# Attention with a mixture of experts on one core: an opening with earlier loads, moved constants, shift rows on another queue and cleared products on TensorE

## The chip, the core and the metric

One core of a Trainium2 chip runs the whole program. The metric is the device time of one execution in microseconds (us), lower is better. The engines are TensorE (PE; its weight loads are listed apart as PEld), VectorE (DVE), ScalarE (ACT), GpSimd (POOL) and SyncE (SP, which here only issues DMAs). ACT also issues DMAs, on a queue of its own.

## The reference

```python
scores = scale * np.matmul(q, k.transpose(0, 1, 3, 2))        # 8 x 8 heads, 576 positions, 64 channels
cum = np.cumsum(np.maximum(s, 0.0), axis=-1)
bias = -(cum[:, :, :, None] - cum[:, :, None, :])
scores = np.where(causal, -1000000000.0, scores + np.minimum(bias, 0.0))
scores = scores - np.max(scores, axis=-1, keepdims=True)
attn = np.exp(scores); attn = attn / (np.sum(attn, axis=-1, keepdims=True) + 1e-09)
x = (attn @ v) with heads side by side, 4608 x 512
# each of the 4608 rows goes to the best of 4 groups and in it to the best of 4 experts
out[rows] = g_w * e_w * (np.maximum(x[rows] @ w1[g, e], 0.0) @ w2[g, e])
```

## The kernel before, in words

The 64 heads are taken in 32 pairs, p = 0 to 31 in the code (so the "fourth pair" is p = 3), and head n belongs to pair n // 2. A step of the main loop of `attention` handles three heads at once: the row maxima of head step + 4 (`rowmax`, `LEAD = 4`), the scores of head step (`scores`) and the product with V of head step - 1 (`av`). Steps -4 to -1 hold only row maxima, step 0 row maxima and scores. The attention is followed by the experts (`moe`), in which TensorE multiplies with weights that are streamed in.

For each pair the raw q and k are loaded (`load_raw`, L159, tile `r`, three buffers). ACT rounds them to fp32r (`split`, L166, tile `hl`), POOL (DVE for p = 0) takes the rests (L170). For the first pairs ACT also writes a part straight into place (`place`, L182). SP then copies the pieces into two operand tiles: `WA` (`load_a`, L191, L193; four buffers) holds rounded q and k and, in rows 64 to 67, sums of s and the shift by the row maximum; `WB` (`load_b`, L203, L204; five buffers) holds the rests. `load_v` (L207) brings V into `VT`, two buffers.

`rowmax` multiplies 66 rows of `WA` on PE (L228) into PSUM tiles `pm`; DVE masks and reduces each (L236) into `mc`. After both heads of a pair, PE transposes `mc` (L250), DVE makes the two shift rows `th` and `tl` (L256, L257) and two DMAs write them to rows 66 and 67 of `WA` (`send`, L262, issued by ACT). Only then can `scores` run for the pair: it multiplies 68 rows of `WA` (L284) and 128 rows of `WB` (L286) into tiles `ps`, ACT takes the exponential (L294), POOL clears the upper triangle (L303), and `av` multiplies with V (L326), whose results ACT copies out (L331, L334).

Each engine executes its own list in order. The lists of PE, DVE, ACT and POOL are written out by hand in strings such as `FIRST` and `ORDERS` (a letter pops one piece of pending work from a queue of that name, B2 is the third piece of the scores); the table `pre` adds loads of the first pairs behind steps -2 to 1. Up to step 0 SP's list is by hand too, later a scheduler places SP's DMAs. A DMA that is issued from SP or ACT takes the next of eight semaphores (DMAHW0 to DMAHW7), and its issuing engine first waits until the earlier DMA on that semaphore has landed:

```python
for r, t in ((66, th), (67, tl)):
    nc.scalar.dma_start(WA[i][r:r + 1, QA]...., t.bitcast(F32))
```

At the start DVE makes the running sums of s (L530 to L534, tiles `cl`, `ch`), and SP copies two rows of them per head into `WA` (L193). Constants of the routing are made by `Router.__init__` on POOL and by `Router.operands` on DVE (L745 to L757), one piece at a time between the row maxima of steps 1 to 3. `hold` adds a wait on another instruction's end, `behind` only an order on the same queue.

Of the kernel before, what the change touches and what calls it, by code (L numbers as in the profile page):

```python
# [121 lines left out]
def attention(tc, qk, v, s, wr, xs, st):  # L122
# [3 lines left out]
    with ExitStack() as ctx:  # L126
# [82 lines left out]
        def rowmax(n):  # L209
# [11 lines left out]
            def item(j, q0, rows, w, c0, cw):  # L221
# [3 lines left out]
                else:  # L225
# [292 lines left out]
        cumd = dr.tile([BH, 2, S], F32, name="cumd")  # L518
        nc.sync.dma_start(s0, s.rearrange("b h s -> (b h) s"))
# [9 lines left out]

        nc.vector.tensor_scalar(out=r1, in0=s0, scalar1=0.0, scalar2=8.0, op0=ALU.max, op1=ALU.mult)  # L530
# [164 lines left out]
class Router:  # L695


    def __init__(self, tc, ac, sm, end, ps_t, ps_s, wr_f, wr_sb, xs, st):
# [35 lines left out]
        n1 = iota("n1", [[S, B], [P, NB]], base=1, cm=1, dt=I32)  # L734
        self.part = ac.tile([P, 2, B, NB], F32, name="part")
        ni = ac.tile([P, B, NB], I32, name="ni")
        self.n1, self.ni, self.uf, self.onesf = n1, ni, uf, onesf
# [1060 lines left out]
```

## Time and profile before

| | |
|---|---|
| median of 3 runs (lowest, highest) | 870.36 us (866.64, 871.6) |
| the profiled execution, its time | 869.25 us |
| its span from first to last instruction | 867.4 us |
| mean granted TensorE clock in it | 0.996 |
| PE busy, PEld busy | 839.2 us (97%), 771.9 us (89%) |
| DVE, ACT, POOL busy | 718.4 us (83%), 615.0 us (71%), 602.5 us (69%) |

The profile shows one execution. Shares of busy time are means over very different stages, so the stages of the opening are read one by one below. [...] DMA share is the mean busy share of the 16 DMA engines, and it can come out slightly above 1.

### The profile page before, as it was taken

The page shows a single profiled execution, that of the slowest core. Times are in us where ns is not written, and L with a number is a line of the kernel's source. Part 1 is how long each engine was busy: PE and PEld are TensorE (multiplying, and loading weights), DVE is VectorE, ACT ScalarE, POOL GpSimd, SP SyncE. Part 2 cuts the span into 40 slices and gives each one's busy share as a digit, 9 for nine tenths or more (in the row PEclk, how much of TensorE's full clock was granted, in tenths as well). Part 3 has the DMA queues.
Part 4 walks back from the last instruction along what each step waited for, and adds up shares of the span by engine and source line. Part 5 has one row for each costly group of instructions (what it writes and reads, how often), then busy time and mean ns, then how long its engine had stood idle before and what let it go on. Part 6 is the DMA issues. An engine that isn't in the chain of part 4 may idle for free. (4 is left out here: it accounts for less than half of the span.)

```text
span 867.4 us, 17805 instructions
## 1 busy us (share of the span) xinstructions
PE 839.2 (97%) x5601; PEld 771.9 (89%) x5601; DVE 718.4 (83%) x1982; ACT 615.0 (71%) x1393; POOL 602.5 (69%) x745
## 2 busy tenths in 40 slices
PE   4989999999999999999999999999999999999997
PEld 2778888888888888887789999999999999999996
DVE  7657788797878889787859799989999999999972
ACT  5668778786878778777747666776677777778760
POOL 9767677676876769545867756776677777777760
PEclk9999999999999999999999999999999999999999
DMA  7899898897979888633646645655566565666620
GB/s 197 266 233 250 234 235 232 213 248 194 248 209 245 236 221 225 177 87 122 194 149 225 245 151 208 205 164 193 201 201 216 188 216 195 223 228 214 215 96 26
DMA packets 82405, 174.06 MB, mean 201 GB/s; under 512 B 9692, under 2 KB 45660, under 8 KB 74112
## 3 DMA queue, kind: packets, MB, share of 16 engines
q1 hardware_dynamic: 72192, 153.20, 60.2%
q0 software_dynamic: 7488, 18.89, 5.7%
q10 hardware_dynamic: 2624, 0.76, 0.4%
q8 instruction: 46, 0.75, 0.3%
q14 instruction: 55, 0.45, 0.2%
HBM read 108.97 MB, written 19.69 MB: 148 GB/s over the span
## 5 line engine op out<-in xcount | busy, mean ns | idle before, releaser
L1067 POOL TENSOR_TENSOR wl<-raw,wh 128x512 fp32r<-128x512 f32 x163 | 209.8, 1299 | 82.5 <-ACT wh L1064 54.6
L236 DVE CUSTOM_DVE_ANT_0 mx<-pm,mask 128x192 bf16<-128x192 f32 (+4 forms) x320 | 127.3, 418 | 33.1 <-PE pm L228 30.4
L1064 ACT CAST wh<-raw 128x512 fp32r<-128x512 f32 x256 | 154.3, 616 | 0.0
L1189 PE MATMUL ph<-xh,wh 128*128 128x256 f32 (+13 forms) x512 | 140.2, 300 | 0.1
L1189 PE MATMUL ph<-xl,wh 128*128 128x256 f32 (+13 forms) x512 | 137.7, 300 | 0.1
L228 PE MATMUL pm<-WA 66*128 66x288 f32 (+4 forms) x384 | 123.8, 355 | 14.0 <-DMA WA<-ch 9.7
L284 PE MATMUL ps<-WA 68*128 68x320 f32 (+4 forms) x384 | 135.4, 356 | 1.7 <-DMA WA<-tl 1.6
L326 PE MATMUL po<-pt,VT 128*128 128x256 f32 (+3 forms) x512 | 119.0, 351 | 3.6 <-POOL pt L303 1.8
L1196 ACT ACTIVATE hh<-ph 128x256 fp32r<-128x256 f32 (+13 forms) x128 | 53.5, 418 | 85.5 <-PE ph L1189 83.3
L1269 PE MATMUL py<-hh,wh 128*128 128x256 f32 (+13 forms) x448 | 113.4, 302 | 0.1
L1269 PE MATMUL py<-hl,wh 128*128 128x256 f32 (+13 forms) x448 | 112.5, 301 | 0.0
L286 PE MATMUL ps<-WB 128*128 128x320 f32 (+4 forms) x384 | 110.2, 300 | 0.0
L1322 DVE STREAM_TRANSPOSE yr<-yT 32x384 f32<-32x384 f32 (+1 forms) x208 | 104.6, 503 | 4.5 <-ACT yT L1266 0.3
L326 PE MATMUL po<-pu,VT 128*128 128x320 f32 (+1 forms) x384 | 105.2, 382 | 0.0
L1159 DVE STREAM_TRANSPOSE xt<-xg 32x256 f32<-32x256 f32 (+1 forms) x208 | 102.3, 492 | 2.7
L326 PEld LDWEIGHTS po<-pt,VT 128*128 128x128 f32 x512 | 87.8, 191 | 16.6 <-POOL pt L303 2.5
L1189 PEld LDWEIGHTS ph<-xh,wh 128*128 128x128 f32 x512 | 95.3, 189 | 0.6 <-DVE hl L1197 0.3
L1189 PEld LDWEIGHTS ph<-xl,wh 128*128 128x128 f32 x512 | 94.7, 189 | 0.5 <-DVE xl L1142 0.3
L1189 PE MATMUL ph<-xh,wl 128*128 128x256 f32 (+13 forms) x512 | 91.9, 299 | 0.0
L170 POOL TENSOR_TENSOR WB<-r,hl 64x576 fp32r<-64x576 f32 x62 | 88.0, 1420 | 5.5 <-ACT hl L166 1.7
L228 PEld LDWEIGHTS pm<-WA 66*128 66x128 f32 (+1 forms) x384 | 68.9, 192 | 24.0 <-POOL WA L528 9.6
L422 POOL TENSOR_TENSOR xTl<-xT,xTh 128x512 fp32r<-128x512 f32 x29 | 37.0, 1275 | 75.9 <-ACT xTh L417 55.7
(255 smaller groups left out, 2001.0 us busy)
## 6 DMA issues: line engine op xcount, KB each, us to landing
raw<-in_w_dram SPq DMA_DIRECT2D x64, 1024.0 KB
r<-in_qk_dram SPq DMA_DIRECT2D x32, 576.0 KB
WA<-hl SPq DMA_DIRECT2D x60, 288.0 KB
WB<-hl SPq DMA_DIRECT2D x60, 288.0 KB
VT<-in_v_dram SPq DMA_DIRECT2D x32, 384.0 KB
WB<-hl SPq DMA_DIRECT2D x64, 144.0 KB
xs<-xr SPq DMA_DIRECT2D x15, 512.0 KB
WA<-cumd SPq DMA_DIRECT2D x56, 4.5 KB
```

The costliest lines, as they stand in the source:

```text
L170: (nc.vector if p < 1 else nc.gpsimd).tensor_tensor(out=hl[:, 2] if part else WB[p % NBB][0:64, KA, h], in0=r[hr, part], in1=hl[hr, part]. ...
L228: nc.tensor.matmul(ps[:rows, :cw], WA[i][0:66, QA, h, QO + q0:QO + q0 + rows], WA[i][0:66, KA, h, QO + c0:QO + c0 + cw], start=True, stop= ...
L236: nc.vector.tensor_tensor_reduce(out=tmp[:rows, :cw], in0=ps[:rows, :cw], in1=mk[:rows], scale=1.0, scalar=-3.0e38 if c0 == 0 else mo, op0 ...
L284: nc.tensor.matmul(ps[:rows, o:o + w], WA[i][0:68, KA, h, QO + k0:QO + k0 + rows], WA[i][0:68, QA, h, QO + q0:QO + q0 + w], start=True, st ...
L286: nc.tensor.matmul(ps[:rows, o:o + w], WB[p % NBB][:, KA, h, k0:k0 + rows], WB[p % NBB][:, QA, h, q0:q0 + w], start=False, stop=True)
L326: nc.tensor.matmul(po[0][:, qa - base:qb - base], VT[p % NVT].rearrange("p t a d -> p (t a d)")[:, (3 * t + 1 + h) * 64:][:, 0:P], x[:, c: ...
L1064: self.casts.append(nc.scalar.copy(h[:, j], raw[:, j]))
L1067: self.low = lows[self.u, i, j] = nc.gpsimd.tensor_tensor(out=l[:, j], in0=raw[:, j], in1=h[:, j].bitcast(F32), op=ALU.subtract)
L1159: V.transpose(dst[:, 0:n, :, j], src[:, 0:n, :, i])
L1189: self.product = nc.tensor.matmul(pss[f][:, :cap], w[f // 4][:, c, (f % 4) * P:(f % 4 + 1) * P], x[:, c, :cap], start=(c == 0 and w is sel ...
L1269: self.product = nc.tensor.matmul(pss[c][:, :cap], w[2 + f // 4][:, f % 4, c * P:(c + 1) * P], x[:, f, :cap], start=(f == 0 and w is self. ...
L1322: V.transpose(dst[:, 0:n, :, i], src[:, 0:n, :, j])
```

## The change

It edits six things, all in the first twelve microseconds of the program or in the first few steps.

- A zero tile `still` is made by DVE, and `stir(n)` multiplies it with itself n times on PE: bf16, 128 rows, 512 columns, into a PSUM tile that nobody reads. 16 such products stand at the head of PE's list, 4 behind ACT's rounding of the sums, and one behind every product of the row maxima of heads 0 to 3.
- The raw load of p = 3 is issued before the `WB` copies of p = 0, its `place` and `split` go ahead of step 0 on ACT, and `load_a(3)` follows its rests.
- The rounding of the sums goes from DVE to ACT, ahead of ACT's other casts; `place(0, 0)` goes behind the two `split` of p = 0.
- The four small DVE operations that make `part` go from steps 2 and 3 to the head of DVE's list, with their POOL input; the casts of `ub` and `ob` go from DVE to ACT.
- The shift rows of p = 2 to 5 (and the second row of p = 0) are issued by SP instead of ACT.
- The `WB` copies of p = 5 wait for an exponential of head 4 and stand behind the `WA` row copies of that pair.

```diff
-                nc.sync.dma_start(w[64:66, KA, h, QO:].bitcast(F32), (cumh if p < 4 else cumd)[n:n + 1].bitcast(F32))
+                st.at["wa", p] = nc.sync.dma_start(w[64:66, KA, h, QO:].bitcast(F32), (cumh if p < 4 else cumd)[n:n + 1].bitcast(F32))
...
+                copies = [nc.sync.dma_start(w[0:64, QA, h], hl[hr, 1])] if h or not placed else []
+                copies.append(nc.sync.dma_start(w[64:128, b, h], hl[hr, 0::2][:, b]))
+                for i in copies if p == 5 else ():
+                    hold(tc, i, st.at["exp", 4])
+                    behind(tc, i, st.at["wa", p])
...
+                if n < LEAD:
+                    stir(1)
...
-                    nc.scalar.dma_start(WA[i][r:r + 1, QA].bitcast(F32).rearrange("o h q -> o (h q)"), t.bitcast(F32))
+                    (nc.sync if (p == 0 and r == 67) or 2 <= p <= 5 else nc.scalar).dma_start(WA[i][r:r + 1, QA].bitcast(F32).rearrange("o h q -> o (h q)"), t.bitcast(F32))
...
+        still = ac.tile([P, P], BF16, name="still")
+        nc.vector.memset(still, 0.0)
+        stirred = ps_o.tile([P, 512], F32, name="stirred", tag="po").rearrange("p (a c) -> p a c", c=P)
+
+        def stir(n):
+            for _ in range(n):
+                i = nc.tensor.matmul(stirred, still, still.unsqueeze(1).to_broadcast([P, 4, P]), start=True, stop=True)
+            return i
+
+        stir(16)
...
+        nc.gpsimd.iota(n1, pattern=[[S, B], [P, NB]], base=1, channel_multiplier=1, allow_small_or_imprecise_dtypes=True)
+        for k, x, op in ((0, 6, ALU.arith_shift_right), (1, 63, ALU.bitwise_and)):
+            nc.vector.tensor_scalar(out=ni, in0=n1, scalar1=x, scalar2=None, op0=op)
+            nc.vector.tensor_copy(part[:, k], ni)
...
-        nc.vector.tensor_copy(cumh[:, 0], c2)
+        rounded = nc.scalar.copy(cumh[:, 0], c2)
+        hold(tc, stir(1), rounded)
+        stir(3)
...
-        pre = {-2: [(load_a, 2, True)],
-               -1: [(load_b, 1, True), (load_v, 0), (load_raw, 3), (load_raw, 4)],
-               0: [(place, 3, 0), (split, 3, 0), (split, 3, 1), (load_a, 3, True), (place, 3, 1), (place, 3, 2), (load_v, 1)],
+        pre = {-2: [(load_a, 2, True), (place, 3, 0), (split, 3, 0, True), (split, 3, 1, True), (place, 3, 1), (place, 3, 2)],
+               -1: [(load_b, 1, True), (load_v, 0), (load_raw, 4)],
+               0: [(need, "G", 3), (load_a, 3, True), (load_v, 1)],
...
-        V.tensor_copy(self.ub, self.uf)
-        yield
-        V.tensor_copy(self.ob, self.onesf)
...
+        self.tc.nc.scalar.copy(self.ub, self.uf)
+        yield
+        self.tc.nc.scalar.copy(self.ob, self.onesf)
```

What stands in the lists now is shown at three places. The first is the head of PE's list, where `pm0` and `pm1` are the row-maximum products of heads 0 and 1. Before, it read:

```order
L228 MATMUL pm0_4_0_235<-WA0_107 128x288
L228 MATMUL pm0_0_0_239<-WA0_107 64x64
L228 MATMUL pm0_1_0_243<-WA0_107 128x192
L228 MATMUL pm0_2_0_247<-WA0_107 128x320
L228 MATMUL pm0_3_0_251<-WA0_107 128x448
```

In the changed kernel the twentieth zero product is followed by these rows (each zero product also loads its weights):

```order
L529 MATMUL stirred_132<-still_130 128x512
L230 MATMUL pm0_4_0_264<-WA0_107 128x288 [waits DMAHW5_49,Activation_49,Pool_49]
L529 LDWEIGHTS still_130
L529 MATMUL stirred_132<-still_130 128x512
L230 MATMUL pm0_0_0_269<-WA0_107 64x64
```

So 16 + 4 zero products stand ahead of the first useful one, and 24 more alternate with the 24 products of heads 0 to 3; behind the last of them nothing of the kind follows.

The second place is SP's list between the `WA` copies of p = 1 and those of p = 2; the digit behind a tile's name is the pair, or for `WA`, `WB` the buffer. Before:

```order
L193 DMA WA1_108<-ch_127 2x1x576 [waits DMAHW2_49]
L204 DMA WB0_111<-hl0_171 64x2x576 [waits DMAHW3_49,DVE_49]
L203 DMA WB0_111<-hl0_171 64x576 [waits DMAHW4_49]
L204 DMA WB0_111<-hl0_171 64x576 [waits DMAHW5_49]
L193 DMA WA2_109<-ch_127 2x1x576 [waits DMAHW6_49,Pool_49]
```

Now:

```order
L193 DMA WA1_108<-ch_127 2x1x576 [waits DMAHW2_49]
L159 DMA r3_223<-in_qk_dram 128x1152 [waits DMAHW3_49,DVE_49,Activation_49]
L203 DMA WB0_111<-hl0_201 64x2x576 [waits DMAHW4_49]
L202 DMA WB0_111<-hl0_201 64x576 [waits DMAHW5_49]
L203 DMA WB0_111<-hl0_201 64x576 [waits DMAHW6_49]
L202 DMA WB2_113<-hl2_252 64x576 [waits DMAHW0_49,Activation_49]
L266 DMA WA0_107<-tl0_332 1x10x128 [waits DMAHW1_49,DVE_49]
L193 DMA WA2_109<-ch_127 2x1x576 [waits DMAHW2_49,Pool_49]
```

The load of p = 3 and one `WB` copy of p = 2 have come in, and the second shift row of p = 0 stands behind them.

The third place is SP's list around the shift rows of p = 3. Before, they stood in ACT's list and SP went from V and the raw load straight on to the `WB` copies of p = 5. Now:

```order
L203 DMA WB4_115<-hl4_543 64x2x576 [waits DMAHW3_49]
L209 DMA VT0_116<-in_v_dram 128x6x128 [waits DMAHW4_49,PE_49]
L159 DMA r7_790<-in_qk_dram 128x1152 [waits DMAHW5_49]
L191 DMA WA1_108<-hl5_625 64x2x576 [waits DMAHW6_49,PE_49]
L193 DMA WA1_108<-cumd_129 2x576 [waits DMAHW7_49]
L159 DMA r8_962<-in_qk_dram 128x1152 [waits DMAHW0_49,Pool_49]
L266 DMA WA3_110<-th3_758 1x10x128 [waits DMAHW1_49,DVE_49]
L266 DMA WA3_110<-tl3_759 1x10x128 [waits DMAHW2_49,DVE_49]
L193 DMA WA2_109<-cumd_129 2x576 [waits DMAHW3_49,PE_49]
L202 DMA WB0_111<-hl5_625 64x576 [waits DMAHW4_49,Activation_49]
```

The two shift rows stand behind the raw load of p = 8 and ahead of the `WB` copies of p = 5.

## Rows read from the trace of the kernel before

**Rows 1.** The page: busy time by engine, and PE in 40 slices.
```profile
PE 839.2 (97%) x5601; PEld 771.9 (89%) x5601; DVE 718.4 (83%) x1982; ACT 615.0 (71%) x1393; POOL 602.5 (69%) x745
...
PE   4989999999999999999999999999999999999997
```

**Rows 2.** Busy time by stretch: stretch, length, PE, PEld, DVE, ACT, POOL, PEclk, DMA share, GB/s.
```profile
9.65:22.20 12.55, 9.35 (x25) 5.87 (x26) 10.63 (x51) 6.64 (x10) 12.07 (x22) 1.00 0.82 200
...
22.20:27.90 5.70, 5.52 (x22) 4.80 (x23) 2.81 (x13) 3.04 (x7) 4.06 (x8) 1.00 1.04 352
27.90:34.40 6.50, 6.50 (x29) 5.76 (x30) 2.55 (x13) 5.03 (x12) 5.50 (x9) 1.00 0.80 234
34.40:41.40 7.00, 6.34 (x36) 4.71 (x34) 6.33 (x18) 4.79 (x12) 5.11 (x8) 1.00 0.90 249
41.40:47.90 6.50, 5.62 (x33) 4.56 (x33) 5.99 (x21) 5.17 (x12) 5.91 (x9) 1.00 0.93 229
47.90:55.35 7.45, 5.65 (x36) 4.74 (x34) 4.43 (x16) 3.10 (x8) 4.24 (x5) 1.00 0.98 239
55.35:62.38 7.03, 7.03 (x37) 6.32 (x37) 3.52 (x14) 6.26 (x16) 3.51 (x6) 0.76 0.90 223
62.38:67.90 5.52, 5.52 (x35) 4.86 (x34) 3.63 (x13) 4.03 (x11) 4.59 (x7) 1.00 0.91 219
```

**Rows 3.** Matmuls by shape, L286 with 448 columns: 22.2 to 31.3, 32 to 52.
```profile
L286 PE MATMUL ps<-WB 128*128 128x448 f32 x1 | 0.6, 575 | 0.0
...
L286 PE MATMUL ps<-WB 128*128 128x448 f32 x4 | 1.5, 369 | 0.0
```

**Rows 4.** Busy time by stretch again, for the 3.35 us behind PE's gap.
```profile
55.35:58.70 3.35, 3.35 (x12) 3.04 (x13) 1.00 (x5) 2.71 (x7) 0.23 (x1) 0.50 0.86 251
```

**Rows 5.** Instructions in order of time, the lead-in: start, us, engine, line, tiles, [idle before].
```profile
4.17 0.50 DVE L530 TENSOR_SCALAR cl<-cl 64x576 f32<-64x576 f32 x1 [4.17 <-DMA cl<-in_s_dram]
...
6.08 0.74 DVE L533 CAST ch<-cl 64x576 fp32r<-64x576 f32 x1
...
6.71 2.41 ACT L166 CAST hl<-r 128x576 fp32r<-128x576 f32 x4
...
9.65 0.95 PE L228 MATMUL pm<-WA 66*128 66x288 f32 x3 [9.65 <-DMA WA<-ch]
```

**Rows 6.** The same view: DVE's set-up operations, first and last of six, and POOL beside them.
```profile
36.58 1.43 DVE L749 CAST ub<-uf 128x128 bf16<-128x128 f32 x1
...
43.42 0.18 DVE L757 CAST part<-ni 128x40 f32<-128x40 int32 x1
...
36.52 2.89 POOL L170 TENSOR_TENSOR WB<-r,hl 64x576 fp32r<-64x576 f32 x2 [1.74 <-ACT hl L166]
```

**Rows 7.** The same view, the shift rows of p = 0 and the first scores.
```profile
18.07 0.74 ACTq L262 DMA_DIRECT2D WA<-tl  x1
...
22.21 0.55 PE L284 MATMUL ps<-WA 68*128 68x256 f32 x1 [1.57 <-DMA WA<-tl]
```

**Rows 8.** The same view, ACT from 16 to 31 us.
```profile
23.01 0.38 ACT L294 ACTIVATE pt<-ps 128x256 f32<-128x256 f32 x1 [6.65 <-PE ps L286]
```

**Rows 9.** The same view, the shift rows of p = 3 and what stands around them.
```profile
46.16 0.49 SPq L203 DMA_DIRECT2D WB<-hl  x1
...
50.44 0.75 ACTq L262 DMA_DIRECT2D WA<-th  x1
...
54.10 0.73 ACTq L262 DMA_DIRECT2D WA<-tl  x1
...
55.35 1.19 PE L326 MATMUL po<-pt,VT 128*128 128x256 f32 x2 [1.80 <-issue]
```

**Rows 10.** DMA issues by line: count in the program, size of one.
```profile
r<-in_qk_dram SPq DMA_DIRECT2D x32, 576.0 KB
WA<-hl SPq DMA_DIRECT2D x60, 288.0 KB
...
VT<-in_v_dram SPq DMA_DIRECT2D x32, 384.0 KB
```

More of the change, by code (lines that the diff above doesn't have):

```diff
@@ L201, in load_b @@
                 b = slice(1 if placed and h else 0, 2)
-                if h or not placed:
-                    nc.sync.dma_start(w[0:64, QA, h], hl[hr, 1])
-                nc.sync.dma_start(w[64:128, b, h], hl[hr, 0::2][:, b])
+                copies = [nc.sync.dma_start(w[0:64, QA, h], hl[hr, 1])] if h or not placed else []
[3 more added lines that the diff above has]
+                    behind(tc, i, st.at["wa", p])
         def load_v(p):
@@ L528, in ones @@
                 nc.gpsimd.memset(WA[i][64:66 if a == QA else 68, a].bitcast(F32).rearrange("p h q -> p (h q)"), 1.0)
+        n1, ni = (ac.tile([P, B, NB], I32, name=n) for n in ("n1", "ni"))
+        part = ac.tile([P, 2, B, NB], F32, name="part")
+        nc.gpsimd.iota(n1, pattern=[[S, B], [P, NB]], base=1, channel_multiplier=1, allow_small_or_imprecise_dtypes=True)
+        for k, x, op in ((0, 6, ALU.arith_shift_right), (1, 63, ALU.bitwise_and)):
+            nc.vector.tensor_scalar(out=ni, in0=n1, scalar1=x, scalar2=None, op0=op)
+            nc.vector.tensor_copy(part[:, k], ni)
         nc.vector.tensor_scalar(out=r1, in0=s0, scalar1=0.0, scalar2=8.0, op0=ALU.max, op1=ALU.mult)
         nc.vector.tensor_tensor_scan(out=c2, data0=r1, data1=r1, initial=0.0, op0=ALU.add, op1=ALU.max)
-        nc.vector.tensor_copy(cumh[:, 0], c2)
+        rounded = nc.scalar.copy(cumh[:, 0], c2)
+        hold(tc, stir(1), rounded)
+        stir(3)
         nc.vector.tensor_tensor(out=cumh[:, 1], in0=c2, in1=cumh[:, 0].bitcast(F32), op=ALU.subtract)
@@ L551, in attention @@
         ones(2)
-        place(0, 0)
         split(0, 0)
         split(0, 1)
+        place(0, 0)
         load_a(0, True)
@@ L561, in attention @@
         load_a(1, True)
+        load_raw(3)
         load_b(0, True)
-        rt = Router(tc, ac, late, end, small, ring, wr_f, wr_sb, xs, st)
+        rt = Router(tc, ac, late, end, small, ring, wr_f, wr_sb, part, xs, st)
         place(1, 1)
@@ L695, with __init__ @@
 class Router:
-    def __init__(self, tc, ac, sm, end, ps_t, ps_s, wr_f, wr_sb, xs, st):
+    def __init__(self, tc, ac, sm, end, ps_t, ps_s, wr_f, wr_sb, part, xs, st):
         self.end = end
@@ L732, in __init__ @@
         nc.gpsimd.iota(st.ie, pattern=[[1, E]], base=0, channel_multiplier=0, allow_small_or_imprecise_dtypes=True)
[L734 to L737, printed above, removed]
+        self.part, self.uf, self.onesf = part, uf, onesf
     def operands(self):
-        V, ni, n1 = self.tc.nc.vector, self.ni, self.n1
+        V = self.tc.nc.vector
         G = self.tc.nc.gpsimd
@@ L743, in operands @@
         G.memset(self.real[64:P, 20:25], 0.0)
-        yield 5
+        yield 6
+        self.tc.nc.scalar.copy(self.ub, self.uf)
+        yield
+        self.tc.nc.scalar.copy(self.ob, self.onesf)
+        yield 4
         V.tensor_copy(self.wr_sb[:, :, 0:20], self.wr_f)
@@ L747, in operands @@
                         op=ALU.subtract)
-        yield
-        V.tensor_copy(self.ub, self.uf)
-        yield
-        V.tensor_copy(self.ob, self.onesf)
-        yield
-        V.tensor_scalar(out=ni, in0=n1, scalar1=6, scalar2=None, op0=ALU.arith_shift_right)
-        V.tensor_copy(self.part[:, 0], ni)
-        yield
-        V.tensor_scalar(out=ni, in0=n1, scalar1=63, scalar2=None, op0=ALU.bitwise_and)
-        V.tensor_copy(self.part[:, 1], ni)
     def step(self, now=False):
```

## The prediction

> **What bounds the kernel now.** I read the page first: PE is busy for 97% of the span, and in 40 slices it is below nine tenths only in the first two and the last [rows 1]. From about 62 us on PE is therefore the bound, and time taken out of the opening passes to the end nearly one for one. The opening is where PE has time to lose, so I read it stage by stage, in the view of busy time by stretch [rows 2], cut at the start of each step's first score or V product.
>
> From 9.65 to 22.20 us only row maxima run: DVE is busy for 10.63 of 12.55 us and sets the pace, PE waits for it. Steps 0 to 5 then take 5.70, 6.50, 7.00, 6.50, 7.45 and 7.03 us, while step 6, the first undisturbed one, takes 5.52 with PE busy throughout. Steps 0 and 1 hold less work than step 6 and yet are longer. What is wrong there is the clock, and the clock column hides it: it says 1.00 from the start, but the same product of 448 columns takes 575 ns in 22.2 to 31.3 us and 369 ns later [rows 3]. In the one stretch where the column does show 0.50, the 3.35 us after PE stood still for 1.80 us [rows 4], the other products also have their slow durations. [...]
>
> **The lead-in, +0.2 us.** The first product waits for the sums' copy until 9.65; DVE starts on s at 4.17 when it lands [rows 5]. The change puts four small DVE operations ahead. They stand among six set-up operations, from 36.58 to 43.42, which take 1.43, 0.78, 1.11, 1.01, 0.94 and 0.18 us; the first ends when POOL's operation beside it does, and the last shows what such an operation takes undisturbed [rows 6]. The four need 0.7 us undisturbed (4 x 0.18) and 3.24 as the trace has them. With a start near 1.4 us (POOL's iota comes first) they end between 2.1 and 4.6 us, so the delay is 0 to 0.5 us; I take 0.2. The rounding costs 0.74 us on DVE and 0.60 on ACT (four casts in 2.41 us) [rows 5], for a second hand-over between engines: 0, with -0.1 to +0.3. `place(0, 0)`, now behind the rounding and two splits, ends near 9.1 us (6.1 + 3 x 0.6 + 1.2 for twice the columns), still ahead of 9.65. The 20 zero products run in PE's idle lead-in: 0.
>
> **The row maxima, +0.4 us.** 24 zero products of 512 columns stand between 24 useful ones. [...] DVE is busy for 10.63 us over four heads, 2.66 each [rows 2]. [...]
>
> **The start of step 0, -1.2 us.** PE waits 1.57 us for the second shift row of p = 0, issued by ACT at 18.07 and landed at 22.2 [rows 7]. On SP it no longer queues behind the first in ACT's list, but behind 720 KB of `WB` copies and a raw load. Those are issued at about 12 to 15 us and should land by 18 to 19 at the 200 to 350 GB/s of that time [rows 2]. 0 to -1.57.
>
> **The clock in steps 0 and 1, -4.1 us.** 9.2 us run at the low clock; at the high one PE needs half, a saving of 4.6 at most. Step 0 then meets DVE (2.81 us busy) and ACT (3.04) [rows 2], so I take 5.70 to 3.35, and 3.5 of step 1's 6.50 us halved: -2.35 - 1.75. This needs the casts of p = 3 out of the way: six times 576 columns, 3.6 us at 0.60 [rows 5]. In steps 0 and 1 ACT is busy for 3.04 + 5.03 = 8.1 us, as long as the two halved steps. They go to ACT's idle 6.65 us ahead of 23.0 [rows 8], if the load of p = 3 has landed by 17 us. If not, they delay the first exponential, and the saving shrinks to 2.
>
> **DVE in steps 2 and 3, -1.5 us.** The six set-up operations (5.45 us) leave DVE, which is busy for 6.33 of 7.00 and 5.99 of 6.50 us. Against 2 x 5.52 the two steps have 2.46 us to give; PE is idle for 1.54 of it [rows 2]. ACT takes two casts of 128 columns, well below 0.6 us each, with over a microsecond free per step. 0 to -2.4.
>
> **The gap at 53.5 us, -3.5 us.** ACT issues the first shift row of p = 3 at 50.44 and the second only at 54.10, and nothing that stands behind it in ACT's list runs before that; PE stops for 1.80 us for lack of what ACT should have cleared [rows 9]. DVE had made both rows by 50.8, so the wait is one for a DMA semaphore: the transfer on it left SP at 46.16 and had 7.9 us to land. That is a backlog on SP's queue. With the rows on SP, ACT is free: -1.85, and PE's 3.35 us at half clock [rows 4] become 1.7: -1.65. 0 (the wait returns elsewhere) to -3.5.
>
> **What is late next, +3 us.** Shift rows on SP stand behind that same backlog. Ahead of those of p = 3 stand, counting from the last `WB` copy of p = 4: 288 KB, V, two raw loads and a `WA` copy, 2112 KB or 2.16 MB [rows 10]. A full DMA moves 244 to 277 GB/s (239 at a share of 0.98, 249 at 0.90), so that is 7.8 to 8.9 us. In the trace the rows are made 2.5 us into step 4 and needed at step 6, 2 x 5.52 - 2.5 = 8.5 us later [rows 2, 9]. This is a draw, with up to 2 us of wait. For p = 4 and 5 another 3.0 to 3.3 MB each come between, 11 to 13.5 us of DMA against 11 us of PE. I take 1 us for each of the three pairs; 0 to 8 in all (2 for the first, up to 3 for each of the others).
>
> [...]
>
> The held copies of p = 5 are 864 KB that no longer stand ahead of these rows; they are needed at step 10, more than 20 us later: 0.
>
> **The sum.** 0.2 + 0.4 - 1.2 - 4.1 - 1.5 - 3.5 + 3 = -6.7 us. The profiled execution took 869.25 us, 1.1 below the median of the runs; 869.25 - 6.7 = 862.6 there, and 870.36 - 6.7 = **863.7 us** against the median.
>
> **The rivals.** A measurement of this kernel can tell about 0.5% (4.4 us) from no change, so faster means below 866.0 and slower above 874.7.
>
> *Shift rows behind the backlog* (0.22). The clock and ACT are won, but pairs 4 to 6 wait for their rows on SP, 8 us together instead of 3: 868.7. For it: the backlog in the trace [rows 9]. Against it: SP's list moves earlier with the rest, and 864 KB are held back. [...]
>
> *DMA paces the opening* (0.12). The DMA share is 0.80 to 1.04 in all stretches from 22 us on, and no byte is saved; PE runs ahead, then waits for V, `WA` or the raw loads, or ACT waits for a semaphore at p = 6, whose rows are still ACT's. All but about 1 us is given back: 869.4. Against it: the share falls to 0.80 in step 1, so there is room [rows 2].
>
> *The zero products hold PE up* (0.08). They don't raise the clock, or it falls in PE's idle 1 to 2 us ahead of the first useful product, as it did behind the gap of 1.80 us. [...]
>
> *All of it, no new wait* (0.13): -6.7 - 3 = -9.7: 860.7.
>
> **How the numbers follow.** My forecast has 0.45, the rivals 0.22, 0.12, 0.08 and 0.13. Faster: 0.45 + 0.13 + a tenth of the first rival, 0.60; slower 0.07; same 0.33. The range of 859 to 870.5 us leaves out the third rival, part of the last and the far end of the second: under 0.2.
>
> **What would show it.** Right: products of 448 columns at 369 ns in the first scores; the first score product near 21 us; no ACT pause between shift rows of p = 3; steps 0 to 5 of about 3.4, 4.8, 6, 6, 6 and 6 us. Wrong: 575 ns there; L228's products waiting behind zero products with DVE idle in the row maxima; PE waits for DMA `WA<-tl` at steps 6, 8 and 10, each of over 2 us; a PE gap that brings the 0.50 back.

## The result and the profile after

The changed kernel takes 877.94 us (median of 8 runs, 872.77 to 879.13), the kernel before 870.98 us on the same chip: a ratio of 1.0072, 95% interval 1.0047 to 1.0096, by the ratio 6.3 us slower (4.1 to 8.4), where 6.7 us faster was forecast. The profiled execution took 879.13 us and is the slowest of the eight; its span is 877.4 us against 867.4 before, so the two traces lie further apart (10.0 us) than the two kernels.

Busy time by stretch in the changed kernel, cut at the starts of the steps like [rows 2] (columns as there):

```profile
9.99:21.11 11.12, 9.83 (x50) 5.28 (x50) 10.48 (x51) 9.65 (x14) 10.70 (x20) 1.00 0.81 196
21.11:25.30 4.19, 3.45 (x21) 2.73 (x21) 2.57 (x13) 3.52 (x8) 4.07 (x6) 1.00 0.81 210
25.30:27.30 2.00, 0.86 (x5) 0.63 (x6) 0.66 (x4) 0.96 (x3) 2.00 (x5) 0.76 1.02 324
27.30:34.39 7.09, 7.09 (x25) 6.15 (x26) 2.06 (x9) 1.89 (x4) 4.91 (x9) 0.59 1.05 271
34.39:41.34 6.95, 6.05 (x36) 4.59 (x34) 3.59 (x16) 6.34 (x16) 4.71 (x6) 1.00 0.88 211
41.34:46.41 5.07, 5.07 (x33) 4.56 (x33) 3.51 (x13) 3.51 (x9) 4.92 (x7) 1.00 0.94 251
46.41:54.33 7.92, 5.81 (x36) 4.84 (x34) 6.52 (x20) 5.11 (x12) 5.22 (x9) 1.00 0.96 229
54.33:61.52 7.19, 5.86 (x36) 4.95 (x37) 3.54 (x14) 5.04 (x13) 3.70 (x6) 1.00 0.85 201
61.52:67.31 5.79, 5.53 (x34) 4.69 (x34) 4.06 (x15) 4.17 (x10) 4.44 (x6) 1.00 0.88 208
67.31:73.18 5.87, 5.87 (x36) 4.92 (x36) 3.92 (x16) 4.64 (x13) 2.94 (x4) 1.00 1.05 234
73.18:77.68 4.50, 0.00 (x1) 0.04 (x1) 0.00 (x0) 0.45 (x2) 0.76 (x3) 0.98 1.06 186
77.68:86.17 8.49, 8.49 (x33) 7.49 (x34) 3.82 (x13) 3.91 (x9) 3.95 (x6) 0.61 0.91 247
```

Step 0 starts at 21.11 us, 1.1 sooner than before, and takes 4.19 us for 5.70. Step 1 (25.30 to 34.39) takes 9.09 for 6.50 and gives all of it back: step 2 starts at 34.39, as before. Step 3 is shorter (5.07 for 6.50), step 4 longer (7.92 for 7.45). In this trace the loss is made in step 7, with 4.50 us in which PE does nothing, and in step 8 behind it, which runs at half clock (granted 0.50) up to 84.0 us and has a mean of 0.61 over its 8.49 us. Before, the same two steps read:

```profile
67.90:73.30 5.40, 5.40 (x39) 4.89 (x37) 4.35 (x18) 4.75 (x14) 2.81 (x6) 1.00 0.87 238
73.30:78.70 5.40, 5.40 (x35) 4.74 (x34) 3.52 (x13) 4.09 (x11) 5.20 (x8) 1.00 1.01 281
```

That is +4.97 and +3.09 us; step 9 starts 7.5 us later than before, and this passes unchanged to the end of the attention.

What PE waits for in 21 to 90 us of the changed kernel (engine, line, tile, what it waits for: us in total, times, longest):

```profile
PE ps L288 <- DMA WA<-tl: 5.8, 2, 4.5
...
PE po L330 <- DMA VT<-in_v_dram: 3.5, 3, 2.1
```

The longest of these waits, in order of time: PE's transpose of the maxima of p = 4, DVE's two shift rows, SP's list, and PE's next score product.

```profile
63.31 0.27 PE L254 MATMUL pmt<-ident,mc 128*10 128x128 f32 x1
...
63.94 0.28 DVE L261 SCALAR_TENSOR_TENSOR tl<-pmt,th 10x128 fp32r<-10x128 f32 x1
...
65.92 0.72 SPq L203 DMA_DIRECT2D WB<-hl  x1
66.69 1.14 SPq L159 DMA_DIRECT2D r<-in_qk_dram  x1
67.93 0.82 SPq L266 DMA_DIRECT2D WA<-th  x1
68.86 0.76 SPq L266 DMA_DIRECT2D WA<-tl  x1
...
77.68 0.55 PE L288 MATMUL ps<-WA 68*128 68x256 f32 x1 [4.50 <-DMA WA<-tl]
```

The row is made at 64.2, issued at 68.86, behind copies and a raw load in SP's list, and PE goes on some 8.8 us later: 13.5 us for 5 KB. (When it landed is taken from the end of PE's wait.)

The clock rose early, as meant, and fell again. Products of 448 columns in 20 to 27 us and in 28 to 33 us (mean ns of one last ahead of the idle time), to be read with [rows 3]:

```profile
L290 PE MATMUL ps<-WB 128*128 128x448 f32 x1 | 0.4, 367 | 0.0
...
L290 PE MATMUL ps<-WB 128*128 128x448 f32 x1 | 0.6, 575 | 0.0
```

Between them PE waits for V of p = 0, which SP issued at 22.31 us, 18.67 before; this is the product it waited with:

```profile
27.30 1.19 PE L330 MATMUL po<-pt,VT 128*128 128x256 f32 x2 [1.09 <-DMA VT<-in_v_dram]
```

### The profile page after: what moved, and what is told of

It reads as the page before. It is cut to its first block, busy times and chain, and to the rows that moved or that the text cites. A ratio compares the mean times of both kernels' runs of the same rounds, so it can differ in the third digit from the quotient of the medians.

```text
span 877.4 us, 17899 instructions
## 1 busy us (share of the span) xinstructions
PE 847.8 (97%) x5645; PEld 773.7 (88%) x5645; DVE 720.7 (82%) x1980; ACT 616.5 (70%) x1396; POOL 600.9 (68%) x745
## 5 line engine op out<-in xcount | busy, mean ns | idle before, releaser
L1081 POOL TENSOR_TENSOR wl<-raw,wh 128x512 fp32r<-128x512 f32 x163 | 209.3, 1296 | 81.8 <-ACT wh L1078 53.5
L1210 ACT ACTIVATE hh<-ph 128x256 fp32r<-128x256 f32 (+13 forms) x128 | 53.5, 418 | 85.8 <-PE ph L1203 84.5
L307 POOL TENSOR_SCALAR_AFFINE_SELECT pt<-pt 128x128 f32<-128x128 f32 (+2 forms) x192 | 65.4, 353 | 37.5 <-ACT pt L298 35.4
```

The lines of the kernel that those rows point to most:

```text
L1081: self.low = lows[self.u, i, j] = nc.gpsimd.tensor_tensor(out=l[:, j], in0=raw[:, j], in1=h[:, j].bitcast(F32), op=ALU.subtract)
```

## The experiments

The theories, as the expectations name them: A, the rows that SP issues stand behind the backlog of its queue; B, the transfers as a whole pace the opening, so that one wait only takes the place of another; C, the zero products cost time; D, the held copies of p = 5 keep SP's list standing; O, the zero products cost by what they change in the scheduler's order of SP's list.

Ratios are to runs of the kernel before on the same chip. The last four columns are from each profiled execution: how much later (+) or sooner (-) than before (36.00, 64.33, 86.17 and 379.10 us) PE transposes the maxima of p = 2, 4, 6 and 30.

| run | ratio (95% interval) | p=2 | p=4 | p=6 | p=30 |
|---|---|---|---|---|---|
| the change | 1.0072 (1.0047, 1.0096) | 0.0 | -1.0 | +7.4 | +7.4 |
| e1 change, rows on ACT | 1.0055 (1.0038, 1.0073) | -0.4 | -3.9 | +2.9 | +2.9 |
| e4 as e1, V sooner | 1.0059 (1.0032, 1.0086) | -2.2 | -1.7 | +4.3 | +4.3 |
| e5 change, no hold | 1.0092 (1.0071, 1.0114) | +0.2 | -3.2 | +4.5 | +4.4 |
| e6 change, old loads of p = 3 | 1.0080 (1.0053, 1.0107) | +1.7 | +1.4 | +4.8 | +4.6 |
| e8 change, no zero products | 1.0018 (0.9998, 1.0038) | -0.4 | -4.4 | -0.9 | -0.4 |
| e9 change, load of p = 6 sooner | 1.0082 (1.0053, 1.0111) | -2.1 | -4.4 | +1.8 | +1.8 |
| e10 change, 20 zero products | 1.0035 (1.0014, 1.0056) | -0.6 | -1.6 | +2.8 | +2.8 |
| e12 as e8, load of p = 6 late | 1.0024 (1.0000, 1.0048) | +0.1 | -3.1 | +3.7 | +3.6 |
| e13 as e8, old loads of p = 3 | 1.0038 (1.0021, 1.0055) | +2.4 | -2.6 | +2.9 | +4.2 |
| e14 as e8, no hold | 1.0015 (0.9998, 1.0032) | -0.8 | -3.7 | -1.4 | -0.2 |
| e2 before, rows of p = 2 to 5 on SP | 0.9971 (0.9953, 0.9989) | -0.2 | -3.9 | -1.6 | -1.6 |
| e18 before, rows of p = 3 on SP | 0.9988 (0.9971, 1.0004) | +0.5 | -3.2 | -2.0 | -2.1 |
| e11 as e2, constants moved | 0.9989 (0.9967, 1.0011) | +1.3 | -3.7 | -3.0 | -2.9 |
| e16 as e2, second row of p = 0 | 1.0034 (1.0016, 1.0051) | +3.2 | -1.2 | +1.4 | +1.4 |
| e3 before, zero products | 1.0028 (1.0009, 1.0047) | -0.2 | -2.2 | -2.2 | -1.6 |
| e7 as e3, one more PSUM tile | 1.0026 (1.0009, 1.0042) | +0.4 | -2.5 | -1.8 | +0.2 |
| e15 as e2, zero products | 1.0024 (1.0006, 1.0042) | +3.2 | -0.4 | +5.4 | +7.0 |
| e17 as e3, 12 more of them | 1.0032 (1.0015, 1.0050) | -0.8 | +2.1 | +2.1 | +2.0 |

Most runs are 1 to 4 us ahead at p = 4, and most of these give part or all of it back by p = 6. From there to p = 30 all but five stay within 0.5 us of where they were.

A profiled execution is one of several, and those of one kernel lie up to 10 us apart (867.06 to 877.07 us in e15). So a trace shows what can happen in a kernel, and only the ratios, which also take out the difference between chips (the kernel before has medians of 868.62 to 870.98 us on them), show what an edit is worth.

### The shift rows: e1, e2, e18

e1 undoes the rows of p = 2 to 5 in the changed kernel (e2 adds them to the kernel before, e18 those of p = 3 alone):

```diff
-(nc.sync if (p == 0 and r == 67) or 2 <= p <= 5 else nc.scalar).dma_start(WA[i][r:r + 1, QA]
+(nc.sync if p == 0 and r == 67 else nc.scalar).dma_start(WA[i][r:r + 1, QA]
```

> The changed kernel with the shift rows of pairs 2 to 5 issued by ACT again, nothing else. Theory A (rows behind the backlog of SP's queue): the wait of 4.50 us at step 8 and the half clock behind it (8.49 us instead of some 5.5) go, 7.5 us together, and ACT's stall between the rows of p = 3 comes back with up to 3.5 us: 870 to 874 us, with PE waiting for a shift row nowhere over 1 us. Theory B (the transfers as a whole pace the opening, whoever issues the rows): PE then waits for V or another copy instead, and the time stays at 876 to 880. Theory C (the zero products cost it): 876 to 880 too, with the waits for shift rows gone from steps 6 and 8 but step 10 starting no sooner than 90 us.

Measured 873.94 us. As a time that is in A's range, but by the ratios (1.0055 against 1.0072) it is 1.5 us below the change, and the intervals overlap: no gain is shown. The wait for a row is gone, but the stall of ACT is back, now at p = 4: it does nothing for 6.31 us. PE stands still behind it for 4.58 us and then runs at half clock (0.57 us for 448 columns at 70.1 us), so one stop has taken the place of the other. ACT and PE in order of time in e1:

```profile
66.65 0.72 ACTq L266 DMA_DIRECT2D WA<-th  x1
67.47 0.72 ACTq L266 DMA_DIRECT2D WA<-tl  x1
68.24 0.38 ACT L338 ACTIVATE sums<-po 64x256 f32<-64x256 f32 x1 [6.31 <-DMA WA<-th]
...
68.72 1.19 PE L330 MATMUL po<-pt,VT 128*128 128x256 f32 x2 [4.58 <-ACT sums L338]
```

> The kernel before with only the shift rows of pairs 2 to 5 moved from ACT to SP. Theory A: ACT's stall of 3.3 us at 50.4 us and the half clock behind it go (-3.5 us), and a wait for a shift row of p = 4, of 3 to 5 us, with half clock for some 8 us behind it, comes in its place (+6 to +8): 873 to 876 us, step 8 waiting for the second row. Theory B: within 1.5 us of the kernel before, 869 to 872, since the rows come as late as the other transfers do. Theory C: faster by the stall, 866 to 868.

Measured 866.88 us, 2.5 below the kernel before by the ratio, as C expected; A is wrong here. ACT's stall is gone, and the longest wait for a row, at step 8, is 1.42 us, with no half clock behind it (granted 1.00 from 71 to 80 us). SP and PE in e2, in order of time:

```profile
63.75 0.76 SPq L262 DMA_DIRECT2D WA<-tl  x1
...
71.25 0.36 PE L284 MATMUL ps<-WA 68*128 68x256 f32 x1 [1.42 <-DMA WA<-tl]
```

The rows are issued 5 us sooner than in the change and land within 7.5 us.

> The kernel before with the shift rows of p = 3 alone on SP. If ACT's stall between the two rows of p = 3, and the half clock behind it, are what the move of the rows gains (prediction's term for the gap at 53.5 us, -3.5): as with the rows of pairs 2 to 5, 866 to 867.5 us. Rival: the stall moves on to the rows of p = 4, still ACT's, as in the changed kernel with its rows back on ACT (6.3 us there): 868 to 871.

Measured 868.47 us, the rival's time, though not by its mechanism: the stall did not move to p = 4 (ACT issues those two rows at 63.32 and 64.17). In the trace it gains 2.1 us by p = 30, e2 1.6, so p = 3 alone can hold the gain, but the ratios don't settle it.

### The zero products: e8, e3, e7, e15, e10, e17

e8 takes all 44 out of the change, e3 adds them to the kernel before:

```diff
-        stir(16)
...
-        hold(tc, stir(1), rounded)
-        stir(3)
...
-                if n < LEAD:
-                    stir(1)
```

> The changed kernel without any zero product, all else as changed. Theory C (the zero products cost it): faster than the changed kernel by 3 us or more, below 875, the operation in the passage to the experts at 0.3 us. Theories A, B and D: steps 0 and 1 run at half clock as before, PE's waits at steps 4, 6 and 8 stay (they are set by transfers), so what the clock lost was hidden behind them: 876 to 880, step 8 starting at 77 to 79 us.

> The kernel before with only the zero products (16 at the head, 4 behind the rounding of the sums, one behind each row-maximum product of heads 0 to 3). Prediction's step on the clock: products of 448 columns at about 370 ns from the first scores on, steps 0 and 1 shorter by up to 4 us, of which ACT's casts of p = 3 (still in step 1) take back 2: 866 to 868.5 us. Theory B: PE then waits for V or the copies of the next pairs and the clock falls again, as at 27.3 us in the changed kernel; 869.5 to 871.5. Theory C: slower, above 872.

Without them the change takes 870.48 us, 0.54% less (1.0072 against 1.0018); alone they make the kernel before 0.28% slower (871.78 us, between the ranges of B and C, and no change lies outside the interval). So the zero products cost time, as C says, and the waits alone (A, B, D) don't explain the loss. How they cost it isn't shown. e3, like the change, is at full clock at first, at half clock behind PE's short stops around step 0 (1.21 us at 21.2, 0.86 at 25.4), and again at 44 us. Its busy time by stretch:

```profile
21.23:27.00 5.77, 4.72 (x29) 3.99 (x30) 3.32 (x16) 3.00 (x7) 5.32 (x11) 1.00 1.00 338
27.00:33.20 6.20, 6.15 (x21) 4.96 (x20) 1.97 (x8) 4.97 (x11) 5.34 (x8) 0.51 0.78 223
33.20:44.00 10.80, 9.24 (x46) 6.70 (x45) 9.16 (x25) 7.21 (x16) 7.46 (x9) 0.97 1.01 249
44.00:47.40 3.40, 3.40 (x13) 3.15 (x14) 2.28 (x10) 2.05 (x5) 2.92 (x5) 0.52 0.83 205
```

Yet e3's trace, of an execution 2.0 us below its median, is not behind in the opening: it is 2.2 us ahead of the kernel before at p = 6 and 1.6 at p = 30, and ends 0.6 us later, so it loses 2.2 us behind the attention. e7, profiled at its median, is 1.8 us ahead at p = 6, 0.2 behind at p = 30 (it loses 2.0 us at p = 18 to 20) and 1.3 at the end. What the zero products cost by themselves is not lost in the opening of these two traces.

In e8, with the same rows on SP, step 8 waits 1.44 us for its row instead of 4.50, and the clock does not fall behind it (1.00 in 71.7 to 80 us):

```profile
71.72 0.36 PE L286 MATMUL ps<-WA 68*128 68x256 f32 x1 [1.44 <-DMA WA<-tl]
```

e7 takes one more tile, so that the V products have their two PSUM buffers in the turn of before:

```diff
+        ps_o.tile([P, 512], F32, name="turned", tag="po")
         stir(16)
```

> The zero products alone, as before, with one more unused PSUM tile taken from the pool of the V products, so that these take its two buffers in the turn of the kernel before. In the run with the zero products alone the attention's end comes 1.5 us sooner than before and 2.2 us are lost again in the passage to the experts, where a VectorE operation of 64 elements takes 3.30 us (0.27 before) beside GpSimd's work. If the turn of the buffers sets that meeting: the operation takes 0.27 to 0.5 us again, and the time is 1.5 to 3 us below the kernel before, 866.5 to 868. If not: as the run with the zero products alone, 870 to 873, the operation at some 3.3 us.

The operation took 0.28 us, but the time is that of e3 (1.0026); and e5 and e6, with the buffers in the turn of the change, have it at 0.27 and 0.28 too. The turn is not the cause; the last section comes back to it.

> The kernel before with the rows of pairs 2 to 5 on SP and all 44 zero products, nothing else. Rows alone: ratio 0.9971; zero products alone: 1.0028 and 1.0026. Theory C as a plain sum (the zero products cost some 2.4 us by themselves): the ratio is within 0.15% of 1.000, 868 to 871 us. Theory A with C (PE, sooner by the clock, only meets the rows on SP sooner, stops there for over 1 us and loses its clock again): more than the sum, 872 to 876, with a wait of 2 us or more for a second shift row at step 6 or 8 and half clock behind it.

Measured 872.47 us, ratio 1.0024, 0.53% above e2 (0.9971). Neither the plain sum (1.000) nor the 872 to 876 us of the other theory is clearly met. In its profiled execution, the slowest of twelve, a wait of 2.4 us for a row at step 8 and half clock behind it are there; the clock had also fallen in the row maxima (0.50 from 11 to 17 us), and step 0 started 3.1 us late:

```profile
76.00:82.00 6.00, 6.00 (x22) 5.33 (x21) 2.58 (x9) 3.14 (x7) 3.73 (x5) 0.50 0.98 261
```

e10 keeps the 20 ahead of the first useful product and drops those among the row maxima.

> The changed kernel with only the 20 zero products ahead of the first useful one, none between the row-maximum products; SP's list is then that of the kernel without zero products but for one swap. Theory O: 868.5 to 872, no wait over 1.5 us at step 8. Theory C: the clock rises at some 4 us and falls within the row maxima or behind the first stops of steps 0 and 1; 872 to 878.

Measured 873.14 us, in C's range, though the interval does not part it from e8. Here the clock fell behind PE's idle 1.75 us ahead of the first useful product, and stayed low. Busy time by stretch in e10:

```profile
11.00:21.30 10.30, 8.17 (x22) 5.15 (x23) 9.80 (x47) 9.08 (x14) 9.88 (x19) 0.50 0.83 198
21.32:31.00 9.68, 9.51 (x35) 8.21 (x36) 4.31 (x22) 4.95 (x12) 9.24 (x14) 0.50 0.76 233
31.00:34.00 3.00, 3.00 (x19) 2.61 (x17) 1.45 (x5) 1.14 (x2) 1.56 (x5) 1.00 1.06 273
```

This is the clock of the kernel before made visible: 0.50 until 31 us, products of 448 columns at 575 ns, 1.00 from there. The step of the prediction that read [rows 3] so was right.

e17 puts 12 more zero products into e3, six of them into PE's stop ahead of the first score:

```diff
-                if n < LEAD:
+                if n < LEAD + 1:
                     stir(1)
...
+            if step == 0:
+                stir(6)
```

> The kernel before with zero products only, now 56 of them: the 44, six more ahead of the first score (in PE's wait for the shift row) and one behind each row-maximum product of step 0; SP's list is that of the kernel before. Theory C with stops (the clock, raised early by zero products, falls behind PE's stops of 1 to 2 us around step 0): the stop at step 0 is filled, the clock does not fall at 25 to 28 us or falls later, and step 2 starts 1 us or more sooner than 34.4 us; 866.5 to 869.5. Rival (the clock falls again whatever stands in the stops, or what it gives is met by later transfers): step 2 starts within 0.7 us of 34.4 and the time stays at 870 to 873.

With the stop filled the clock did not fall at 25 to 28 us in the profiled execution, which speaks for the stop as the cause of that fall. Step 2 starts 0.8 us sooner than before, between the two expectations, and the time is the rival's, 872.05 us: ACT then does nothing for 5.44 us around the rows of p = 3, PE stops for 3.70 us, and 5.8 us at half clock follow. Busy time by stretch in e17:

```profile
21.34:29.40 8.06, 8.01 (x49) 5.75 (x47) 4.93 (x24) 4.47 (x9) 5.66 (x10) 1.00 0.95 293
29.40:34.67 5.27, 3.94 (x25) 3.51 (x26) 2.03 (x9) 4.07 (x11) 4.99 (x9) 1.00 0.75 227
52.50:56.22 3.72, 0.02 (x2) 0.03 (x1) 0.64 (x4) 0.45 (x2) 0.00 (x0) 0.90 1.02 229
56.22:62.00 5.78, 5.78 (x22) 5.47 (x23) 1.65 (x5) 4.56 (x12) 2.25 (x5) 0.50 1.05 257
```

### SP's list: e9, e12

With zero products the scheduler also puts the raw load of p = 6 later in SP's list, behind the shift rows of p = 2 (issued at 40.26 us, 33.88 in e8). e9 asks for that load one step sooner in the change; e12 holds it back in the kernel without zero products:

```diff
-               1: [(split, 4, 0), (split, 4, 1), (load_b, 2, True), (load_raw, 5)]}
+               1: [(split, 4, 0), (split, 4, 1), (load_b, 2, True), (load_raw, 5), (load_raw, 6)]}
```

> The changed kernel with all its zero products, but the raw load of p = 6 asked for one step sooner, so that SP issues it ahead of the operand copies of p = 4 (about where it stands without zero products) and not behind the shift rows of p = 2. Theory O (the 44 zero products cost by what they do to the scheduler's order of SP's list: the load of p = 6 comes 6 us later, and with it all behind it): the rows of p = 4 are issued at some 64 us instead of 67.9, step 8 waits under 1.5 us instead of 4.50: 868 to 872 us. Theory C (the zero products cost by the clock, which rises early but then falls to half behind every short stop of PE): the half clock from some 27 to 33 us stays, a stop of 1 to 2 us later brings it back once more, and the time stays above 874.

```diff
+            if p == 6:
+                behind(tc, i, st.at["rows", 2])
```

> The changed kernel without zero products (870.5 us), but with the raw load of p = 6 held behind the shift rows of p = 2, as in SP's list of the changed kernel; the two lists then differ by one 4.5 KB copy. Theory O: the loss comes back without any zero product: rows of p = 4 issued at 67 us or later, PE waits 3 us or more for them at step 8, 874 to 878. Theory C: as without the hold, 869 to 872.

e9: 876.80 us, ratio 1.0082, no better than the change, though in its trace, 3.3 us below its median, the wait at step 8 shrank to 2.58 us; e12: 872.79 us, 1.0024 against e8's 1.0018. So O is a small part at most. In e12's profiled execution it did bring a wait of 2.79 us for the row at step 8.

### Loads, hold, the first row, the constants: e4, e5, e6, e13, e14, e16, e11

e4 loads V of p = 0 sooner in e1:

```diff
-        pre = {-2: [(load_a, 2, True),
+        pre = {-2: [(load_v, 0), (load_a, 2, True),
```

> As the run with the rows on ACT, and V of p = 0 loaded ahead of the row and operand copies of p = 2 and the WB copies of p = 1. Theory A with a clock that falls behind any short gap of PE: PE's wait of 1.09 us at 27.3 us goes, and with it the half clock up to 33 us (7.09 us for what takes some 4.5 at full clock); step 2 starts 2 to 3.5 us sooner than 34.4 us, and the time is 1 to 3.5 us below that of the run with the rows on ACT. Theory B: PE waits for the copies of p = 1 or 2 instead and the time is within 1 us of that run.

Step 2 starts 2.2 us sooner, as A expected, and the time is the same as e1's (874.46 us, 1.0059 against 1.0055), as B expected.

e5 (and e14, without zero products) takes the hold away:

```diff
-                for i in copies if p == 5 else ():
-                    hold(tc, i, st.at["exp", 4])
-                    behind(tc, i, st.at["wa", p])
```

> The changed kernel without the wait and the order on the WB copies of p = 5, all else as changed. Theory D (the held copies, which SP's list cannot pass, push V, operand copies and the shift rows of p = 4 behind them later and into one bunch): the rows of p = 4 are issued at some 63 us instead of 67.9, the wait of 4.50 us at step 8 and the half clock behind it (8.49 us instead of some 5.5) shrink to under 1.5 us together, V of p = 2 no longer costs 2.11 us: 868 to 872 us. Theory A (any rows on SP behind the backlog): 288 to 864 KB more stand ahead of the rows of p = 3 and 4, the waits at steps 6 and 8 stay or grow: 876 to 880.

> The changed kernel without zero products and without the hold on the WB copies of p = 5; the earlier load of p = 3 stays. Theory D: 867 to 869 us, with the rows of p = 4 waiting under 1 us. Theory A (every KB on SP ahead of the rows makes them later): the waits for rows at steps 6 and 8 grow to 2 us or more, with half clock behind them: 871 to 875. Theory B: as without zero products, 870 to 872.

876.18 and 870.27 us: no difference beyond the intervals in either, and in e5's trace step 8 still waits 4.87 us for its row. Theory D falls.

e6 (and e13, without zero products) puts the raw load, casts and placing of p = 3 back:

```diff
-        load_raw(3)
...
+               -1: [(load_b, 1, True), (load_v, 0), (load_raw, 3), (load_raw, 4)],
+               0: [(place, 3, 0), (split, 3, 0), (split, 3, 1), (load_a, 3, True), (place, 3, 1), (place, 3, 2), (load_v, 1)],
```

> The changed kernel with the raw load, the casts and the placing of p = 3 where they stood before, all else as changed (rows on SP, copies of p = 5 held, zero products). Theory B (the earlier load of 576 KB makes V and the rows of p = 0 and all behind them late): V of p = 0 lands in time, PE does not wait 1.09 us at 27.3 us and its clock does not fall there, but ACT's casts (3.6 us) delay exponentials of step 1; step 2 starts 1 to 2.5 us sooner than 34.39 us. If theory D holds as well, the wait at step 8 stays near 4.5 us and the time is 875 to 878; if the wait at step 8 comes of the earlier load, it is under 1.5 us and the time 868 to 872.

> The changed kernel without zero products and with the raw load, casts and placing of p = 3 where they stood before; what is left of the change is the rows on SP, the held copies of p = 5 and the moved constants and roundings. Without zero products alone it was 1.6 us above the kernel before (ratio 1.0018), with rows and constants only 1.0 below. Theory B (the earlier load costs by making V and the copies of p = 1 and 2 late): 867 to 869 us, at or below the kernel before. Theory D (the hold costs): as without zero products, 870 to 872.

875.44 us with zero products, 872.79 without (1.0038 against 1.0018): the intervals overlap in both pairs, so no cost of the earlier load is shown. Theory B, that this load is what makes the others late, falls. In e6's trace PE doesn't wait for V in step 1, but it stops there for 1.14 us for POOL, and half clock follows all the same (0.50 in 28.9 to 34 us).

e16 adds the second row of p = 0 on SP to e2:

```diff
-(nc.sync if 2 <= p <= 5 else nc.scalar)
+(nc.sync if (p == 0 and r == 67) or 2 <= p <= 5 else nc.scalar)
```

> The kernel before with the shift rows of pairs 2 to 5 and the second row of p = 0 on SP, as the change has them, nothing else. Prediction's term for the start of step 0 (-1.2 us, 0 to -1.57): step 0 starts at 20.5 to 21.3 us instead of 21.6 to 22.2, and the time is 0.5 to 1.2 us below that with the rows of pairs 2 to 5 alone, 865.5 to 866.5 where that was 866.9. Rival (the opening is paced by the transfers, so an earlier step 0 waits later): within 0.5 us of it.

Measured 871.58 us: 0.63% slower than e2, where a gain or a tie was expected. In its trace step 0 no longer waits for the row, but ACT reaches its cast of p = 3 before the raw load has landed, stands there, and PE transposes the maxima of p = 2 3.2 us late. That this is the cause was not tried apart. ACT in e16:

```profile
28.06 1.15 ACT L182 CAST WA<-r 64x1152 fp32r<-64x1152 f32 x1 [1.94 <-DMA r<-in_qk_dram]
```

e11 adds the constants to e2: the four DVE operations at the head, the two casts on ACT.

> The kernel before with two parts of the change only: the shift rows of pairs 2 to 5 on SP, and the constants (the four small DVE operations at the head, two casts on ACT). With the rows alone it was 2.6 us below the kernel before. Prediction's term for the constants (-1.5 us in steps 2 and 3): 865 to 867, with steps 2 and 3 shorter by 1 to 2 us. Rival: PE then only waits for the next transfer, and it is the same as with the rows alone, 866 to 868; or the later start of the sums (0.3 us) and two more casts on ACT cost up to 1 us.

868.67 us: no gain over e2, if anything a loss.

## Why the prediction was wrong

Where -6.7 us were forecast, the change's trace is 7.5 us late at step 9: the start of step 0 gives -1.1, steps 0 and 1 +1.1, steps 2 and 3 -1.5, steps 4 and 5 +0.6, step 6 +0.3, steps 7 and 8 +8.1.

**What bounds the opening.** The first step failed for the opening itself: what is taken out of one stage there does not pass on "nearly one for one", it is met by a wait in a later stage, and in the changed kernel PE stops for 4.50 us at 73 us, where it was to be the bound from 62 us on. From step 9 on the rule holds: the change is 7.4 us late at p = 6 and at p = 30. From the first useful product to the start of step 8, busy time by stretch reads so before, in the change and in e2:

```profile
9.65:73.30 63.65, 56.93 (x280) 46.50 (x280) 44.26 (x173) 42.81 (x96) 47.80 (x75) 0.97 0.90 238
```

```profile
9.99:77.68 67.69, 55.42 (x304) 43.38 (x304) 40.90 (x167) 45.27 (x100) 48.38 (x75) 0.95 0.93 222
```

```profile
9.48:71.25 61.77, 55.89 (x279) 45.44 (x280) 44.31 (x173) 43.67 (x97) 48.97 (x77) 1.00 0.96 240
```

Length times rate gives 15.1, 15.0 and 14.8 MB, and 14.7, 14.8 and 14.6 MB in e8 (61.73 us at 238 GB/s), e10 (64.64 at 229) and e16 (64.77 at 226): step 8 starts when about the same bytes have moved, at a DMA share of 0.90 to 0.96. The equal bytes say little, since each variant must move them to get there; the high share, and e4 and e16, where an earlier stage brought no gain, speak for the rival "DMA paces the opening". PE's busy time does not set the pace: the change has less of it than before and arrives 4 us later. But the share does not tell the time either (the change has 0.93 at 222 GB/s, e2 0.96 at 240), so what limits the transfers stays open. The rival had 0.12 and was priced as a gain of 1 us; as far as its reading is right, its price was not, because a stop that moves can also grow (1.80 us before, 4.50 in the change).

**The clock in steps 0 and 1, -4.1: one of the two terms that failed most.** The two steps take 13.28 us, 12.20 before: +1.1 where -4.1 was forecast. The clock is as low before as the prediction read it, and the zero products do raise it (products of 448 columns at 367 ns in the first scores, 575 before). That PE needs half at the high clock no run shows; before, the next product starts 0.37 us after the one of 448 columns at 24.35 us and 0.21 us after the one at 31.83. But the changed kernel's PE then outruns V by 1.09 us and loses the clock for some 6 us (0.50 from 27.3 to 33 us), and step 2 starts when it did. As runs, the zero products alone measured +0.28% (2.4 us slower) and in the change, by their absence, +0.54% (4.7 us); in the traces of e3 and e7 about 2 us of the forecast gain are there at p = 6 and gone by the end. The prediction named such a fall among the signs of being wrong ("a PE gap that brings the 0.50 back") and gave it no price.

**The row maxima, +0.4.** No run shows the +0.4 as a term of its own. Measured were 11.12 us against 10.98 (12.55 less the wait of 1.57): near it in this execution, and partly luck: in e6 and e15 the clock fell within them (in e15 0.50 from 11 to 17 us), and the first transpose of p = 0 came at 18.04 and 17.71 us instead of 15.60.

**The lead-in, +0.2, and the start of step 0, -1.2.** 9.99 us for 9.65, and 21.11 for 22.21: right as times, but by e16 the start of step 0 alone is worth nothing; in its trace ACT then waits for the load of p = 3.

**DVE in steps 2 and 3, -1.5.** The two steps take 12.02 us for 13.50, as said; e11 shows no gain in the total.

**The gap at 53.5, -3.5.** ACT's stall and the half clock behind it went (1.00 in both steps). PE waits 2.11 us for V instead, and steps 4 and 5 take 15.11 us for 14.48: +0.6 where -3.5 was forecast.

**What is late next, +3 (0 to 8): the other one.** The wait came where it was expected, but not in its size: 4.97 us in step 7 and 3.09 in step 8, 8.1 us for p = 4 alone in this trace, where 1 us was taken (for p = 3 PE waited 1.33). The prediction counted the wait and not the half clock behind it (0.50 from 77.7 to 84.0 us). It also missed the 4.6 us in which the finished rows stand in SP's list before they are issued. From the row's issue to the end of the wait another 8.8 us go by; in what order a queue moves what it was given no run shows. By itself the move of the rows does not lose: in the kernel before it gains 2.5 us (e2), where ACT's stall goes and a row that lands in 7.5 us costs PE 1.42 us.

**What stays open.** The zero products cost 0.27% on the kernel before and 0.54% on e8; the intervals are too wide to say whether the rows on SP make them dearer. How they cost it stays open too: in the change's trace it is the stops and the half clock behind them, in those of e3 and e7 the time goes behind p = 6.

## What to carry to other kernels

Before a stage is credited with PE's idle or slow time, look at its DMA share: at 0.90 to 0.96 up to step 8, an earlier V (e4) and an earlier first row (e16) brought nothing, and what gained was a move that freed ACT (e2, share 0.96 for 0.90). Price a stop of PE together with the half clock that may follow it (here 4.5 us and 3.1 more). Of the edits only the shift rows on SP were shown to gain by themselves: 866.88 us, 0.29% below the kernel before. The earlier load and the hold were not run alone on it.

## What the hardware showed that was not expected

The clock that cleared products raise was lost again in the opening in the traces of the change (0.50 from 27.3 to 33 us), e3 (0.51 in 27 to 33.2), e10 (0.50 in 11 to 31), e15 (0.50 in 11 to 17) and e17 (0.50 in 12 to 14). If the clock is taken to be either 1.00 or 0.50, as in most stretches here, a run's mean granted clock gives an estimate of the time at half clock that its records show, 2 x (1 - clock) x span: with the change's 0.992 some 14 us, 6 of them in the 7.09 us behind the stop for V (0.59) and 7 in the 8.49 us behind the stop of 4.50 us (0.61). But the size of a stop did not decide alone: the change kept the clock (1.00) behind 1.76 us at 10.0 us, where e10 lost it (0.50 from 11 us) behind 1.75; e10 itself kept it (1.00) behind 1.98 us at 48.6 us, e16 (1.00) behind 1.90 at 74.5, and the change lost it (0.50) with the 1.09 us ahead of 27.3.

A small VectorE operation lasted, in the change, until a run of GpSimd operations ended. In the passage to the experts one of 64 elements a partition takes 0.27 us before and 3.24 in the change. Instructions in order of time, DVE and POOL, before and in the change:

```profile
460.99 0.27 DVE L674 SCALAR_TENSOR_TENSOR idl<-lists 128x64 f32<-128x64 f32 x1
...
461.34 2.55 POOL L1067 TENSOR_TENSOR wl<-raw,wh 128x512 fp32r<-128x512 f32 x2 [1.18 <-ACT wh L1064]
```

```profile
464.73 6.28 POOL L1081 TENSOR_TENSOR wl<-raw,wh 128x512 fp32r<-128x512 f32 x5
...
467.91 3.24 DVE L697 SCALAR_TENSOR_TENSOR idl<-lists 128x64 f32<-128x64 f32 x1
```

Before, GpSimd is idle there; in the change it runs five operations without a break, and the VectorE operation ends 0.1 us behind the last of them. In 8 of the 20 profiled executions it takes 3.2 to 3.3 us, in 12 it takes 0.27 to 0.56; the 8 are 7 of the 11 with zero products and 1 of the 9 without (e12). The change's trace loses another 2.6 us between p = 30 (+7.4) and its end (+10.0), where this stands. Measured so against the kernel before, the 8 executions lose 1.9 to 3.0 us there, and the other 11 between -1.0 and +1.1. So this may be part of what the zero products cost; no run took it away by itself, and whether they bring it about is not shown.
